# A four-layer attention and MLP kernel: VectorE and GpSimd exchange work, each GpSimd step tied to a VectorE sum, and the order plan spares time after transfers

## The chip, the cores and the metric

The kernel runs on one core of a Trainium2 chip. The metric is the device time of one execution in microseconds (us); three runs of the kernel before gave 1188.9 us as their median (1188.76 to 1190.28).

## The reference

```python
x = A_x                                               # 1 x 2048 x 640
x = x + A(layernorm(x), wqkv, wo)                     # attention, 32 heads of 20
x = x + B(layernorm(x), w1, b1, w2, b2)               # B has a layernorm of its own
x = x + A(layernorm(x), wqkv, wo)                     # the same weights again
x = x + B(layernorm(x), w1, b1, w2, b2)
# A: q, k, v = x @ wqkv; every position attends to itself and to 7 earlier ones, 2 apart;
#    softmax over these 8; the weighted sum of v; then @ wo
# B: gelu(y @ w1 + b1) @ w2 + b2, with 1536 hidden columns
```

## The kernel before, in words

**Units.** The even and the odd positions never meet in the attention, so the 2048 rows are cut into four units of 512 rows (two of even, two of odd positions). Two layers make eight units, n = 0 to 7; units 4 to 7 are the second layer. A unit has four row tiles t and four head groups g (8 heads, 160 columns each).

**Products in two halves.** Every fp32 operand of a product is split into a high and a low fp16 half, and each product is three fp16 passes on TensorE. ScalarE rounds the high half; the low half is a subtraction of 640 elements per partition, as a rule on VectorE: line 506 for the normalised rows `hl`, line 653 for the attention's result `ohl`, lines 720 and 849 for the hidden rows.

**Stages of a unit.** (1) The layernorm: sums on ScalarE, a power of -0.5 on GpSimd (line 487), low halves (line 506), then a transposing DMA into `yT` (line 511). (2) The product with `wqkv` (line 539), evicted by ScalarE into `ev` (three buffers) and put into DRAM in another layout by a DMA from ScalarE's queue (line 551); it is fetched again by SyncE (line 570). (3) The attention of each group on VectorE: products of q and k in two halves of 2560 elements (line 606), each summed by a TENSOR_REDUCE (line 610), the softmax (lines 615 to 625), the products with v (line 632), three adding steps (lines 640 and 644) into the one buffer `o`, then the high half (line 651, ScalarE) and the low half (line 653). (4) After the fourth group, four transposing DMAs (line 661) and the projection with `wo` (line 672, 120 matmuls, called the project below); VectorE adds it to x (line 678). (5) The second layernorm, and the bias b2 added to x (line 515, VectorE, 640 elements for each of the 32 tiles). (6) The MLP: the first product (line 709), gelu and halves (lines 715, 718, 720), the second product (lines 728 and 731), and the sum into x (line 751).

**The last two units.** For units 6 and 7 the second MLP product is done in a Strassen form with seven products instead of eight (`mlp_fast`): first products at line 834 (180 matmuls a unit), seven products at line 900 (252 matmuls a unit), sums into x at line 919. It needs sums of weights, made once by `prep_sums` (line 776: 24 operations of 320 elements and 6 of 1280, on GpSimd), and sums of hidden rows (line 854: 24 operations of 256 elements a unit; unit 6 on GpSimd, unit 7 on VectorE).

**What sets the order.** All steps are handed to a `Plan` with an engine, a duration, a priority, what they need and give, and the buffers that they use. `Plan.run` plays them through once on the host, always takes the step that can start first (with ties by priority), and the kernel then emits them in order of their planned start. Each engine works through its own list in that order on the chip; a step that is late there holds all that stands behind it. DMA commands stand in such lists too: SyncE's list (SP) holds nearly all, ScalarE's the puts (line 551) and the split weights on their way to DRAM (24 `mw` transfers, line 410 now).

Of the kernel before, what the change touches and what calls it, by code (L numbers as in the profile page):

```python
# [45 lines left out]

FAST_OUT = (6, 7)
# [16 lines left out]
class Plan:  # L64
# [12 lines left out]

    PATIENCE = 0.7
# [12 lines left out]
    def add(self, eng, dur, prio, emit, need=(), give=(), use=(), table=None, move=0.0, lazy=False):  # L91
        o = dict(eng=eng, dur=dur, prio=prio, emit=emit, need=need, give=give, use=use, table=table,
                 move=move, lazy=lazy, n=len(self.ops))
        self.ops.append(o)
        for u in use:
            if u not in self.users and u[0] in self.ORDERED and u not in self.line.setdefault(u[0], []):
                self.line[u[0]].append(u)
            self.users[u] = self.users.get(u, 0) + 1

    def run(self):  # L100
# [13 lines left out]
        order = []  # L114

        def start(o):
# [3 lines left out]
            for k in o["need"]:  # L120
                e, w = when[k]
                w = w + (self.LAG[e] if e != o["eng"] else 0.06 * (e != "pe"))
                t = max(t, w)
            new = {}
            for u in o["use"]:
                if u in self.slot:
                    t = max(t, self.since[u])
                else:
# [7 lines left out]
                    new[u[0]] = i + 1  # L136
            return t

        total = len(self.ops)
        while len(order) < total:  # L140
# [19 lines left out]
            d = o["dur"]  # L160
            if o["table"] and o["table"] != table:
# [23 lines left out]
            for k in o["give"]:  # L185
                when[k] = (e, end)
# [19 lines left out]
def sliding_dilated_then_mlp_kernel(  # L206
# [76 lines left out]
    T["g"] = [b[:, :NS * HT2].rearrange("p (s c) -> p s c", s=NS) for b in (act_buf, ev_buf)]  # L283
# [27 lines left out]
    def dve(n, prio, emit, need=(), give=(), use=(), more=0.0):  # L311
        plan.add("dve", v_cost(n) + more, prio, emit, need, give, use)
# [3 lines left out]

    def dma(kb, prio, emit, need=(), give=(), use=(), by="sp"):
        lazy = give[0][0] in ("x", "sq", "st", "c1", "c2", "zero", "mw", "tr", "ms", "fw") or give[0] in ("b1", "b2")
        plan.add(by, 0.1 if by == "act" else 0.38, prio, emit, need, give, use, move=kb / 330.0, lazy=lazy)

    def dma_transpose(prio, emit, need=(), give=(), use=()):
        plan.add("sp", 1.45, prio, emit, need, give, use, move=1.4)
# [5 lines left out]
    def constants():  # L328
        nc.vector.memset(half, -0.5)
# [6 lines left out]
    def mask_value():  # L336
        nc.vector.tensor_scalar(mask, mask, 0.0, -1e9 / scale, op0=OP.is_lt, op1=OP.mult)
# [67 lines left out]
    def prep_m(f, i, prio):  # L405
# [4 lines left out]
        dma(328, prio - 5, lambda: nc.scalar.dma_start(mw[i][f], tile_of(*ck)),  # L410
            need=[("lo", ("m", f, i))], give=[("mw", f, i)], use=[ck], by="act")

    def turn(prio, t, name, hk, yk):

        for a in range(2):
# [27 lines left out]
    def layernorm(n, prio, yk, twice):  # L443
# [13 lines left out]
        for t in range(m if fast else 0):  # L457
            def stats(t=t):
# [3 lines left out]
                nc.vector.tensor_scalar_add(bn[:, t, 13:14], bn[:, t, 13:14], EPS)  # L462
# [19 lines left out]
        for t0 in range(0, 0 if fast else m, cut):  # L482
# [4 lines left out]
            pool(2.5, prio, lambda t0=t0, t1=t1: nc.gpsimd.tensor_tensor(  # L487
# [6 lines left out]
        for t in range(m):  # L494
# [19 lines left out]
            if twice:  # L514
                dve(D, -350, lambda t=t: nc.vector.tensor_add(x[u][:, t], x[u][:, t], b2),  # L515
                    need=[("y", name, t), ("fg", n, 2, 0) if n in FAST_OUT else ("hhi", at(n, t) * NF + 2 * t + 2), "b2"], give=[("xb", n, t)])

# [3 lines left out]
    def qkv(n):  # L521
# [6 lines left out]
        for k, (g, b) in enumerate(halves):  # L528
            ek = ("ev", (n, g, b))
            for i in range(2):  # L530
# [12 lines left out]
                mm(3 * KD * 3 * GC, 15, -500 + n + 0.01 * k, product,  # L543
# [5 lines left out]
            def put(g=g, b=b, ek=ek):  # L549
                to = spill[la][par]  # L550
                nc.scalar.dma_start(
# [5 lines left out]
                give=[("put", n, g, b)], use=[ek], by="act")  # L557
# [20 lines left out]
    def attention(G):  # L578
# [21 lines left out]
        for a in range(NE):  # L600
# [3 lines left out]
            def qk(t0=t0, pk=pk):  # L604
                w = tile_of(*wk)
                nc.vector.tensor_mul(tile_of(*pk), w[:, HALO + m + t0:HALO + m + t0 + EH, None, :].to_broadcast([P, EH, W, GC]),  # L606
# [5 lines left out]
                axis=AX.X, op=OP.add), need=[("qk", G, a)], give=[("lg", G, a)], use=[pk, sk])  # L612
# [14 lines left out]
        for a in range(NE):  # L627
# [3 lines left out]
            def pv(t0=t0, vk=vk):  # L631
                nc.vector.tensor_mul(  # L632
# [15 lines left out]
        def hi():  # L648
# [4 lines left out]
        dve(m * GC, -300 + G, lambda: nc.vector.tensor_sub(tile_of(*hk)[:, :, 1, g * GC:(g + 1) * GC], tile_of(*ok), hi()),  # L653
            need=[("oh", G)], give=[("ol", G)], use=[ok, hk])

    def project(n):
# [7 lines left out]
        for t in range(m):  # L664
            for c in range(2):
# [10 lines left out]
                def residual(t=t, c=c, pk=pk):  # L676
                    xs = x[u][:, t, c * D // 2:(c + 1) * D // 2]
                    nc.vector.scalar_tensor_tensor(xs, tile_of(*pk)[:, :D // 2], 1.0 / WS, xs, op0=OP.mult, op1=OP.add)  # L678
# [8 lines left out]
    def mlp(at, b, t0, t1):  # L687
# [61 lines left out]
        def residual(c0, c1, i0, i1, src):  # L749
            xt = x[u][:, i0:i1, c0:c1]  # L750
            nc.vector.scalar_tensor_tensor(xt, src, 1.0 / WS, xt, op0=OP.mult, op1=OP.add)
# [10 lines left out]
    def prep_sums(j, prio):  # L762
# [12 lines left out]
        def add(o, a, b, op):  # L775
            nc.gpsimd.tensor_tensor(o, a, b, op=op)  # L776
# [5 lines left out]
        def t1():  # L782
            b11, b12, b21, b22, tf = blocks_of()
            add(tf[:, 1], b12, b11, OP.subtract)

        def t3():
            b11, b12, b21, b22, tf = blocks_of()
            add(tf[:, 2], b22, b12, OP.subtract)

        def t2():  # L790
            b11, b12, b21, b22, tf = blocks_of()
            add(tf[:, 0], b22, tf[:, 1], OP.subtract)

        def t4():
            b11, b12, b21, b22, tf = blocks_of()
            add(tf[:, 3], b21, tf[:, 0], OP.subtract)
# [4 lines left out]
        for name, f, need in (("1", t1, both), ("3", t3, both), ("2", t2, [("ts", j, "1")]), ("4", t4, [("ts", j, "2")])):  # L801
            pool(1.0, prio, f, need=need, give=[("ts", j, name)], use=[key])
        act(4 * HD, -300, lambda: nc.scalar.activation(parts()[2][:, :, 0], parts()[1], AF.Copy),
            need=[("ts", j, "4"), ("ts", j, "3")], give=[("th", j)], use=[key])
        pool(3.2, prio, lambda: add(parts()[2][:, :, 1], parts()[1], parts()[2][:, :, 0], OP.subtract),
             need=[("th", j)], give=[("tl", j)], use=[key])
# [4 lines left out]
    def mlp_fast(at, b):  # L811
# [4 lines left out]
        free = [("out", b - 1, NF - 1, i) for i in range(M)] if b - 1 not in FAST_OUT else []  # L816
        free += [("ms", q, j) for q in SUMS for j in range(HF)] + [("put", N - 1, g, i) for g in range(NG) for i in range(2)]
# [4 lines left out]
        for jj in range(HF):  # L822
            gk, hk = ("g", (b, jj)), ("h", (b, jj))
            for s in range(2):
# [20 lines left out]
            def split_h(half, low, gk=gk, hk=hk):  # L845
                s0, s1 = ((0, 3), (3, NS))[half]
                to = tile_of(*hk)[half]
                if low:
                    nc.vector.tensor_sub(to[:, 1], gs(gk, s0, s1), to[:, 0])
# [3 lines left out]
            def add(o, a, c, op, gk=gk):  # L853
                (nc.vector if b == N - 1 else nc.gpsimd).tensor_tensor(tile_of(*gk)[:, o], tile_of(*gk)[:, a], tile_of(*gk)[:, c], op=op)
# [3 lines left out]
            for i, (o, a, c, op) in enumerate(((4, 3, 1, OP.add), (5, 4, 2, OP.subtract), (6, 0, 5, OP.subtract), (3, 2, 3, OP.subtract))):  # L858
                f = lambda o=o, a=a, c=c, op=op, f=add: f(o, a, c, op)
                if b == N - 1:  # L860
# [139 lines left out]
```

## Time and profile before

| | us |
|---|---|
| median of 3 runs | 1188.9 |
| the profiled execution | 1189.57 |
| its span, first to last instruction | 1187.8 |
| TensorE (PE) busy | 1153.7 |
| VectorE (DVE) busy | 1063.6 |
| ScalarE (ACT) busy | 538.3 |
| GpSimd (POOL) busy | 153.0 |

Busy times are of the span. PE waits in the trace are idle times ahead of an instruction, put down to what came last. A row of the timeline has its start, its length, the engine, the line, what it writes and reads, how many like it follow each other, and in brackets the idle time ahead of it.

### The profile page before, as it was taken

What the parts mean: (1) busy time and instruction counts of PE and PEld (TensorE: products, weight loads), DVE (VectorE), ACT (ScalarE), POOL (GpSimd) and SP (SyncE); (2) the same over time, 40 slices, a digit from 0 to 9 for tenths busy, and PEclk for the clock granted to TensorE, in tenths of its full rate; (3) what the DMA queues carried; (4) which work ended last, traced back from release to release, by engine and by line L of the source; (5) the groups of instructions that cost most, each with busy time, mean ns of one, the idle gap of its engine ahead of it and who ended that gap; (6) DMA issues with size and microseconds to landing.
All of it is one profiled execution on the core that took longest, in us unless ns stands there. A gap on an engine that the chain in (4) does not pass through costs nothing.

```text
span 1187.8 us, 17373 instructions
## 1 busy us (share of the span) xinstructions
PE 1153.7 (97%) x6844; PEld 632.0 (53%) x6844; DVE 1063.6 (90%) x1030; ACT 538.3 (45%) x939; POOL 153.0 (13%) x100
## 2 busy tenths in 40 slices
PE   7999999999979999999999999999998799989998
PEld 4444446577544565545554455546454555447556
DVE  7899999999999999999998999989999999873361
ACT  6476444535283435732637253364343552344240
POOL 1011000001010000000002010022055440450000
PEclk9999999999999999999999999999999899989999
DMA  9998999889675558577565757568766894546645
GB/s 303 289 314 271 309 328 279 244 264 289 172 218 161 175 170 205 164 195 207 153 199 150 203 152 210 182 159 175 212 237 238 231 241 130 183 100 187 182 124 173
DMA packets 235758, 248.77 MB, mean 209 GB/s; under 512 B 131148, under 2 KB 185756, under 8 KB 235676
## 3 DMA queue, kind: packets, MB, share of 16 engines
q1 hardware_dynamic: 206620, 208.34, 61.5%
q10 hardware_dynamic: 29056, 39.33, 9.5%
q8 instruction: 53, 0.87, 0.3%
q14 instruction: 29, 0.24, 0.1%
HBM read 168.76 MB, written 48.71 MB: 183 GB/s over the span
## 4 chain that ended last, share of the span: by engine, by line
PE 66%; DVE 21%; issue 6%; POOL 3%; ACT 2%; DMA 2%; SPq 0%; DVEq 0%; POOLq 0%; ACTq 0%
PE ps L539 25%; PE ps L709 12%; PE acc L728 9%; PE ps L672 8%; PE acc L900 6%; DVE pr L606 4%; DVE pr L632 4%; PE ps L834 3%; DVE pr L640 3%; DVE sm L610 3%; PE acc L731 2%; POOL ln L487 2%; DVE act L720 2%; DVE xf L515 1%; DVE hl L506 1%
## 5 line engine op out<-in xcount | busy, mean ns | idle before, releaser
L539 PE MATMUL ps<-wq,yT 128*128 128x480 f16 x1920 | 392.6, 367 | 0.0
L539 PEld LDWEIGHTS <-yT 128*128 128x128 f16 x1920 | 187.9, 98 | 201.2 <-issue 1.5
L709 PE MATMUL ps<-yT,c 128*128 128x512 f16 (+1 forms) x1260 | 248.8, 351 | 6.4 <-DMA yT<-hl 6.4
L728 PE MATMUL acc<-c,act 128*128 128x512 f16 x864 | 240.4, 379 | 2.4 <-DVE act L720 2.3
L632 DVE TENSOR_TENSOR pr<-sm,v 128x2560 f32<-128x2560 f32 x64 | 182.4, 2868 | 0.0
L709 PEld LDWEIGHTS <-c 128*128 128x128 f16 x1260 | 120.7, 98 | 114.7 <-issue 9.9
L606 DVE TENSOR_TENSOR pr<-qk 128x2560 f32<-128x2560 f32 x64 | 179.6, 2807 | 0.1
L610 DVE TENSOR_REDUCE sm<-pr 128x128 f32<-128x2560 f32 x64 | 179.6, 2806 | 0.0
L731 PE MATMUL acc<-c,act 128*128 128x128 f16 x864 | 178.6, 219 | 0.9 <-DVE act L720 0.9
L487 POOL TENSOR_TENSOR ln<-ln,half 128x2 f32<-128x2 f32 (+1 forms) x30 | 58.2, 1938 | 761.1 <-ACT ln L484 761.1
L672 PE MATMUL ps<-wo,yT 128*128 128x320 f16 x960 | 136.7, 305 | 14.2 <-DMA yT<-ohl 12.4
L545 ACT ACTIVATE ev<-ps 128x480 f32<-128x480 f32 x128 | 72.3, 566 | 170.3 <-PE ps L539 169.9
L640 DVE TENSOR_TENSOR pr<-pr 128x640 f32<-128x640 f32 (+1 forms) x128 | 148.7, 1184 | 0.0
L728 PEld LDWEIGHTS <-act 128*128 128x128 f16 x864 | 84.2, 98 | 101.0 <-DVE act L720 3.7
L672 PEld LDWEIGHTS <-yT 128*128 128x128 f16 x960 | 95.4, 100 | 55.9 <-DMA yT<-ohl 14.2
L715 ACT ACTIVATE act<-ps,b 128x512 f32<-128x512 f32 (+1 forms) x84 | 52.1, 623 | 156.4 <-PE ps L709 148.1
L731 PEld LDWEIGHTS <-act 128*128 128x128 f16 x864 | 82.0, 98 | 8.9 <-DVE act L720 1.0
L834 PE MATMUL ps<-yT,c 128*128 128x512 f16 x360 | 78.5, 379 | 0.4 <-ACT act L840 0.3
L470 ACT ACTIVATE junk<-xf 128x640 f16<-128x640 f32 x56 | 41.2, 735 | 81.6 <-DVE xf L678 71.4
L720 DVE TENSOR_TENSOR act<-act 128x512 f16<-128x512 f32 (+1 forms) x84 | 58.0, 693 | 15.2 <-ACT act L718 15.1
L776 POOL TENSOR_TENSOR wq<-wq 128x320 f32<-128x320 f32 (+1 forms) x30 | 56.4, 1898 | 67.8 <-ACT wq L798 47.4
L900 PE MATMUL acc<-c,wq 128*128 128x320 f16 x420 | 61.8, 299 | 0.0
(82 smaller groups left out, 942.0 us busy)
## 6 DMA issues: line engine op xcount, KB each, us to landing
c<-mw SPq DMA_DIRECT2D x192, 320.0 KB, 3.4
spill<-ev ACTq DMA_DIRECT2D x64, 480.0 KB, 4.2
qk<-spill SPq DMA_DIRECT2D x32, 880.0 KB, 6.2
v<-spill SPq DMA_DIRECT2D x32, 880.0 KB, 4.9
qk<-spill SPq DMA_DIRECT2D x32, 320.0 KB, 4.0
mw<-c ACTq DMA_DIRECT2D x24, 320.0 KB, 4.7
c<-msp SPq DMA_DIRECT2D x24, 320.0 KB, 3.5
act<-in_B_w_dram SPq DMA_DIRECT2D x21, 320.0 KB, 5.6
```

Source lines behind the costliest of these rows:

```text
L487: pool(2.5, prio, lambda t0=t0, t1=t1: nc.gpsimd.tensor_tensor(col(2)[:, t0:t1], col(2)[:, t0:t1], half[:, t0:t1], op=OP.pow), need=[("vr" ...
L539: nc.tensor.matmul(ps, transposed(yk)[:, a * KD + k, t * P:(t + 1) * P], wq[:, b, k, g], start=j == 0, stop=j == 3 * KD - 1)
L606: nc.vector.tensor_mul(tile_of(*pk), w[:, HALO + m + t0:HALO + m + t0 + EH, None, :].to_broadcast([P, EH, W, GC]), windows(w, t0, [GC, W], ...
L610: dve(E, G - 0.7, lambda pk=pk, t0=t0: nc.vector.tensor_reduce(lg(t0, t0 + EH).rearrange("p t w h -> p (t w h)"), tile_of(*pk).rearrange(" ...
L632: nc.vector.tensor_mul(tile_of(*vk).rearrange("p t w (h d) -> p t (w h) d", d=DH), lg(t0, t0 + EH).rearrange("p t w h -> p t (w h)")[:, :, ...
L640: dve(EH * w * GC, G - 0.9, lambda vk=vk, w=w: nc.vector.tensor_add(tile_of(*vk)[:, :, 0:w], tile_of(*vk)[:, :, 0:w], tile_of(*vk)[:, :, w ...
L672: nc.tensor.matmul(tile_of(*pk)[:, :D // 2], transposed(yk)[:, a * KD + k, t * P:(t + 1) * P], wo[:, b, k, c * D // 2:(c + 1) * D // 2], s ...
L709: nc.tensor.matmul(tile_of(*pk)[:, :nt], tile_of(*ck)[:, a, k * P:(k + 1) * P], transposed(yk)[:, c * KD + k, t0 * P:t1 * P], start=i == 0 ...
L728: nc.tensor.matmul(acc[i], w, tile_of(*wk)[:, c, :BANK], start=e == 0 and (a, c) == PASS[0], stop=end, skip_group_check=True)
L731: nc.tensor.matmul(acc[4][:, i * P:(i + 1) * P], w, tile_of(*wk)[:, c, BANK:], start=e == 0 and i == t0 and (a, c) == PASS[0], stop=end, s ...
L834: nc.tensor.matmul(tile_of(*pk), tile_of(*ck)[:, a, k * P:(k + 1) * P], transposed(yk)[:, c * KD + k, :], start=i == 0, stop=i == 3 * KD - 1)
L900: nc.tensor.matmul(acc[bank][:, :HD], tile_of(*hk)[half][:, a, slot, t * P:(t + 1) * P], load()[:, z, c], start=q in FIRST and i == 0 and ...
```

## The change

The edits, none of which alters what is computed:

1. **GpSimd to VectorE.** The 30 sums of weights (line 776 before, 815 now) and the 24 sums of hidden rows of unit 6 (line 854 before, 894 now) go to VectorE.
2. **VectorE to GpSimd.** The low half of `ohl` for groups 0 to 2 of each unit (24 of 32; line 653 before, 689 now) and the bias additions of units 0 to 6 (28 of 32; line 515 before, 548 now) go to GpSimd.
3. **Ties.** Such a step (`laid`) is planned into a window: the time of a TENSOR_REDUCE of line 610 (646 now). It then waits, by an added dependency, for the VectorE instruction just ahead of that sum, so that it starts when the sum starts. If no window is to be had in time, it is planned without a tie. Of the 52 steps 46 are tied; not tied are one bias addition of unit 0, the four of unit 6 and the low half of group 2 of unit 7.
4. **Spared time.** In the plan a TensorE step that needs a transfer counts it as landed 0.5 us later, and 2.0 us later for a transposing DMA.
5. **Queues.** The 64 puts and the 24 `mw` transfers go from ScalarE's queue to SyncE's.
6. **Smaller ones.** The first product of unit 4 gets a late priority; the planned length of the power on GpSimd is 3.0 instead of 2.5; the two buffers `g` of the Strassen form change places, so that the first of them needn't wait for unit 5's outputs.

```diff
+SPARE = (0.5, 2.0)
...
+        def window(o, t):
+            for w in windows:
+                if o["beside"] > w[3]:
+                    continue
+                s = max(t, w[0])
+                if s + o["dur"] <= w[1] + self.OVER:
+                    return s, w
+            return None, None
...
-                w = w + (self.LAG[e] if e != o["eng"] else 0.06 * (e != "pe"))
+                w = w + (self.LAG[e] if e != o["eng"] else 0.06 * (e != "pe")) + spare * (o["eng"] == "pe")
...
+                if o["opens"]:
+                    shut -= 1
+                    windows.append([t + 0.2, t + d, ahead, o["opens"]])
+                    del windows[:-4]
...
-    T["g"] = [b[:, :NS * HT2].rearrange("p (s c) -> p s c", s=NS) for b in (act_buf, ev_buf)]
+    T["g"] = [b[:, :NS * HT2].rearrange("p (s c) -> p s c", s=NS) for b in (ev_buf, act_buf)]
...
+    def laid(n, prio, emit, until, need=(), give=(), use=(), level=1):
+        plan.add("pool", 0.17 + n / 450.0, prio, emit, need, give, use, beside=level, until=until)
...
-                mm(3 * KD * 3 * GC, 15, -500 + n + 0.01 * k, product,
+                mm(3 * KD * 3 * GC, 15, (-500 + n if n != NU else 24 + 11 * b) + 0.01 * k, product,
...
-                nc.scalar.dma_start(
+                nc.sync.dma_start(
...
-        dve(m * GC, -300 + G, lambda: nc.vector.tensor_sub(tile_of(*hk)[:, :, 1, g * GC:(g + 1) * GC], tile_of(*ok), hi()),
-            need=[("oh", G)], give=[("ol", G)], use=[ok, hk])
+        low = lambda by: by.tensor_tensor(tile_of(*hk)[:, :, 1, g * GC:(g + 1) * GC], tile_of(*ok), hi(), op=OP.subtract)
+        if g < NG - 1:
+            laid(m * GC, -300 + G, lambda: low(nc.gpsimd), lambda ready, when: any(("o", G + 1) in q["use"] for q in ready.get("dve", ())), need=[("oh", G)], give=[("ol", G)], use=[ok, hk])
+        else:
+            dve(m * GC, -300 + G, lambda: low(nc.vector), need=[("oh", G)], give=[("ol", G)], use=[ok, hk])
...
-            nc.gpsimd.tensor_tensor(o, a, b, op=op)
+            return nc.vector.tensor_tensor(o, a, b, op=op)
...
     for o in plan.run():
-        o["emit"]()
+        o["ins"] = o["emit"]()
+        if o["behind"]:
+            tc.add_manual_dep(o["ins"].ins, o["behind"]["ins"].ins.name, mybir.DependencyInfo(
+                mybir.DependencyClass.Sync, mybir.DependencyReason.DATA), reason="order")
```

GpSimd's list near the last units, before: powers of layernorms (`ln`), then the sums of weights (`wq` is the buffer that these share).

```order
L487 TENSOR_TENSOR ln_91<-ln_91,half 128x2 x2
L487 TENSOR_TENSOR ln_90<-ln_90,half 128x2 x2
L487 TENSOR_TENSOR ln_89<-ln_89,half 128x2 x2
L487 TENSOR_TENSOR ln_91<-ln_91,half 128x2 x2
L487 TENSOR_TENSOR ln_90<-ln_90,half 128x2 x2
L776 TENSOR_TENSOR wq<-wq 128x320 x4
L776 TENSOR_TENSOR wq<-wq 128x4x320
```

GpSimd's list now, at its end: low halves (`ohl`) and bias additions (`xf`) between the last powers.

```order
L548 TENSOR_TENSOR xf<-xf,b_103 128x640
L520 TENSOR_TENSOR ln_89<-ln_89,half 128x2 x2
L548 TENSOR_TENSOR xf<-xf,b_103 128x640
L689 TENSOR_TENSOR ohl_73<-o_86,ohl_73 128x4x160
L548 TENSOR_TENSOR xf<-xf,b_103 128x640
L689 TENSOR_TENSOR ohl_73<-o_86,ohl_73 128x4x160
L548 TENSOR_TENSOR xf<-xf,b_103 128x640 x5
L689 TENSOR_TENSOR ohl_73<-o_86,ohl_73 128x4x160
L520 TENSOR_TENSOR ln_91<-ln_91,half 128x2 x2
```

The sums have left GpSimd; powers of layernorms now stand behind tied steps, and the last low half of GpSimd stands behind five bias additions.

VectorE's list at the last group of unit 7 before: products with v and adding steps (`pr`, `o`), between them low halves and bias additions of unit 6 (`wq`, `xf`), and the last low half of the attention (`ohl`), on which the project of unit 7 waits.

```order
L632 TENSOR_TENSOR pr_75<-sm_88,v_69 128x2560
L849 TENSOR_TENSOR wq<-act,wq 128x768
L849 TENSOR_TENSOR wq<-act,wq 128x1024
L640 TENSOR_TENSOR pr_74<-pr_74 128x2x640
L640 TENSOR_TENSOR pr_75<-pr_75 128x2x640
L849 TENSOR_TENSOR wq<-ev,wq 128x768
L849 TENSOR_TENSOR wq<-ev,wq 128x1024
L515 TENSOR_TENSOR xf<-xf,b_103 128x640 x4
L849 TENSOR_TENSOR wq<-act,wq 128x768
L849 TENSOR_TENSOR wq<-act,wq 128x1024
L640 TENSOR_TENSOR pr_74<-pr_74 128x2x320
L640 TENSOR_TENSOR pr_75<-pr_75 128x2x320
```

The same place now, up to the last low half and the first steps behind it (`acc` are PSUM banks of unit 5).

```order
L790 SCALAR_TENSOR_TENSOR xf<-acc_98,xf 128x512
L676 TENSOR_TENSOR pr_75<-pr_75 128x2x320
L676 TENSOR_TENSOR pr_74<-pr_74 128x2x640
L680 TENSOR_TENSOR o_86<-pr_75 128x320
L676 TENSOR_TENSOR pr_74<-pr_74 128x2x320
L680 TENSOR_TENSOR o_86<-pr_74 128x320
L689 TENSOR_TENSOR ohl_73<-o_86,ohl_73 128x4x160
L894 TENSOR_TENSOR ev<-ev 128x256 x4
L889 TENSOR_TENSOR wq<-ev,wq 128x768
L889 TENSOR_TENSOR wq<-ev,wq 128x1024
```

The low halves of unit 6 and its bias additions no longer stand ahead of the last low half. On TensorE the project of unit 7 stood behind all 180 first products (line 834) of unit 6; now it stands behind 75 of them, and the other 105 follow it. The project of unit 6 stood behind the first products of three hidden blocks of unit 5 (45 matmuls of line 709) and 30 pairs of second products (lines 728 and 731) that now follow it.

More of the change, by code (lines that the diff above doesn't have):

```diff
@@ L76 @@
     LAND = 1.0
+    OVER = 0.3
     PATIENCE = 0.7
@@ L89, in __init__, with add @@
         self.line = {}
-    def add(self, eng, dur, prio, emit, need=(), give=(), use=(), table=None, move=0.0, lazy=False):
+    def add(self, eng, dur, prio, emit, need=(), give=(), use=(), table=None, move=0.0, lazy=False, spare=0.0,
+            opens=0, beside=0, until=None):
         o = dict(eng=eng, dur=dur, prio=prio, emit=emit, need=need, give=give, use=use, table=table,
-                 move=move, lazy=lazy, n=len(self.ops))
+                 move=move, lazy=lazy, spare=spare, opens=opens, beside=beside, until=until, behind=None, ins=None, n=len(self.ops))
         self.ops.append(o)
@@ L114, in run @@
         order = []
+        windows = []
+        shut = sum(o["opens"] > 0 for o in self.ops)
+        ahead = None
+        def window(o, t):
[6 more added lines that the diff above has]
+            return None, None
         def start(o):
@@ L136, in start @@
                     new[u[0]] = i + 1
+            if o["beside"] and (shut or windows):
+                s, _ = window(o, t)
+                return s if s is not None or shut and not o["until"](ready, when) else t
             return t
@@ L160, in run @@
             d = o["dur"]
+            if o["beside"]:
+                _, w = window(o, t)
+                if w:
+                    w[0] = t + d + 0.1
+                    o["behind"] = w[2]
+            if e == "dve":
+                if o["opens"]:
+                    shut -= 1
+                    windows.append([t + 0.2, t + d, ahead, o["opens"]])
+                    del windows[:-4]
+                ahead = o
             if o["table"] and o["table"] != table:
@@ L328, in constants @@
     def constants():
-        nc.vector.memset(half, -0.5)
+        return nc.vector.memset(half, -0.5)
     dve(8, -900, constants, give=["half"])
@@ L556, in qkv @@
             dma(P * 6 * GC * 4 / 1e3, -310 + n, put, need=[("ev", n, 2 * b + i, g) for i in range(2)],
-                give=[("put", n, g, b)], use=[ek], by="act")
+                give=[("put", n, g, b)], use=[ek])
     def fetch(G):
@@ L815, in mlp_fast @@
         ready = [("yT", ("b", b), t) for t in range(M)]
-        free = [("out", b - 1, NF - 1, i) for i in range(M)] if b - 1 not in FAST_OUT else []
-        free += [("ms", q, j) for q in SUMS for j in range(HF)] + [("put", N - 1, g, i) for g in range(NG) for i in range(2)]
+        free = [("ms", q, j) for q in SUMS for j in range(HF)] + [("put", N - 1, g, i) for g in range(NG) for i in range(2)]
         def gs(k, s0, s1):
@@ L823, in mlp_fast @@
             gk, hk = ("g", (b, jj)), ("h", (b, jj))
+            if jj == 1 and b - 1 not in FAST_OUT:
+                free += [("out", b - 1, NF - 1, i) for i in range(M)]
             for s in range(2):
```

66 lines of the change are left out of this document (33 added, 33 removed).

## The prediction

> **What bounds the kernel now.** I read the page's busy times first, then TensorE's waits, then the timeline at the longest of them.
>
> ```profile
> PE 1153.7 (97%) x6844; PEld 632.0 (53%) x6844; DVE 1063.6 (90%) x1030; ACT 538.3 (45%) x939; POOL 153.0 (13%) x100
> ```
>
> TensorE is busy for 97% of the span, and the change neither adds nor removes a matmul. All that can be won is TensorE's idle time, with what hangs on it.
>
> ```profile
> PE ps L672 <- DMA yT<-ohl: 12.4, 3, 6.8
> PE ps L709 <- DMA yT<-hl: 6.4, 1, 6.4
> PE acc L728 <- DVE act L720: 2.3, 3, 0.9
> PE ps L672 <- DVE xf L678: 1.8, 1, 1.8
> PE acc L731 <- DVE act L720: 0.9, 1, 0.9
> PE ps L834 <- ACT act L840: 0.3, 1, 0.3
> ```
>
> Each row: who waited for whom, us in total, times, the longest. They sum to 24.1 us; the start-up, which the change hardly touches, has the rest. The largest part is the project (line 672), which waits for the transposed low halves of the attention three times. The timeline of TensorE shows these waits in brackets, and the same work without a wait for comparison (the first row, and the last one, from the chain of work that ended last).
>
> ```profile
> 192.59 16.46 PE L672 MATMUL ps<-wo,yT 128*128 128x320 f16 x120
> 355.11 7.12 PE L709 MATMUL ps<-yT,c 128*128 128x512 f16 x22 [6.43 <-DMA yT<-hl]
> 680.14 10.12 PE L672 MATMUL ps<-wo,yT 128*128 128x320 f16 x72 [1.63 <-DMA yT<-ohl]
> 925.33 8.39 PE L672 MATMUL ps<-wo,yT 128*128 128x320 f16 x45 [6.83 <-DMA yT<-ohl]
> 1057.62 18.98 PE L672 MATMUL ps<-wo,yT 128*128 128x320 f16 x120 [3.89 <-DMA yT<-ohl]
> 1114.14 35.61 PE ps L834 x165
> ```
>
> After a long wait TensorE also runs slow for a while. A project's 120 matmuls take 16.46 us with no wait ahead of them and 18.98 behind the 3.89 us wait: 2.5 us lost. The 45 behind 6.83 us take 8.39 instead of 45 x 16.46 / 120 = 6.2: 2.2 lost. The 22 behind 6.43 us take 7.12 instead of 22 x 35.61 / 165 = 4.7: 2.4 lost. The 72 behind 1.63 us take 10.12 against 9.9: nothing. The granted clock (the column before the last two) shows it:
>
> ```profile
> 315.00:430.00 115.00, 107.67 (x638) 58.44 (x637) 111.76 (x106) 55.08 (x94) 3.49 (x3) 0.97 0.64 186
> 900.00:960.00 60.00, 51.30 (x316) 28.95 (x315) 60.00 (x53) 29.94 (x50) 32.13 (x17) 0.94 0.84 248
> ```
>
> So the waits cost 24.1 + 7.1 = 31.2 us, and that is the ceiling of any gain. [...]
>
> The second row of that answer also shows VectorE busy for all 60 us. It is the partner that TensorE waits for: the low half of the last group of a unit ends its attention.
>
> ```profile
> 1053.27 0.83 DVE L653 TENSOR_TENSOR ohl<-o,ohl 128x640 f16<-128x640 f32 x1 [0.80 <-ACT ohl L651]
> ```
>
> It starts at 1053.27 and the project at 1057.62, 4.35 us later, by way of the transposing DMA. The question is how much earlier VectorE gets there, and how much earlier TensorE.
>
> **VectorE's list, part by part.** Groups by line and shape: count, busy us, mean ns of one, idle time ahead.
>
> ```profile
> L653 DVE TENSOR_TENSOR ohl<-o,ohl 128x640 f16<-128x640 f32 x32 | 27.6, 862 | 3.0 <-ACT ohl L651 3.0
> L515 DVE TENSOR_TENSOR xf<-xf,b 128x640 f32<-128x640 f32 x32 | 29.2, 925 | 0.0
> L644 DVE TENSOR_TENSOR o<-pr 128x320 f32<-128x320 f32 x64 | 32.7, 521 | 0.0
> L849 DVE TENSOR_TENSOR wq<-act,wq 128x1024 f16<-128x1024 f32 x6 | 7.3, 1223 | 5.5 <-ACT wq L851 5.5
> L849 DVE TENSOR_TENSOR wq<-act,wq 128x768 f16<-128x768 f32 x6 | 6.8, 1125 | 0.0
> L854 DVE TENSOR_TENSOR act<-act 128x256 f32<-128x256 f32 x12 | 4.8, 423 | 6.4 <-ACT act L840 6.2
> L506 DVE TENSOR_TENSOR hl<-y,hl 128x640 f16<-128x640 f32 x64 | 51.4, 818 | 7.3 <-ACT hl L504 7.3
> L720 DVE TENSOR_TENSOR act<-act 128x512 f16<-128x512 f32 x60 | 48.2, 804 | 14.0 <-ACT act L718 13.9
> L720 DVE TENSOR_TENSOR act<-act 128x256 f16<-128x256 f32 x24 | 9.7, 416 | 1.3 <-ACT act L718 1.2
> L632 DVE TENSOR_TENSOR pr<-sm,v 128x2560 f32<-128x2560 f32 x64 | 182.4, 2868 | 0.0
> L606 DVE TENSOR_TENSOR pr<-qk 128x2560 f32<-128x2560 f32 x64 | 179.6, 2807 | 0.1
> ```
>
> Ahead of the last low half of unit 7, VectorE loses 24 low halves, 24 x 0.862 = 20.7 us; 28 bias additions, 28 x 0.925 = 25.9; and three pairs of low halves of unit 6's hidden rows, which now stand behind it, 3 x (1.125 + 1.223) = 7.0. It gains 24 weight sums of 320 elements, priced at the row of that shape, 24 x 0.521 = 12.5, and 6 of 1280, by the 1024 row scaled up, 6 x 1.53 = 9.2. The 24 sums of hidden rows (24 x 0.424 = 10.2) stand behind it, beside TensorE's own work, and I cost them at nothing (10.2 if that cover fails). Net: 53.6 - 21.7 = 31.9 us earlier.
>
> **The contention that goes.** Some operations of VectorE are stretched while GpSimd makes its sums, others not. GpSimd's timeline, then VectorE's:
>
> ```profile
> 861.47 3.45 POOL L776 TENSOR_TENSOR wq<-wq 128x320 f32<-128x320 f32 x4 [31.50 <-ACT wq L798]
> 867.15 4.16 POOL L776 TENSOR_TENSOR wq<-wq 128x1280 f16<-128x1280 f32 x1 [2.23 <-ACT wq L803]
> 899.91 2.62 POOL L776 TENSOR_TENSOR wq<-wq 128x1280 f16<-128x1280 f32 x1 [1.38 <-ACT wq L803]
> 861.90 2.81 DVE L610 TENSOR_REDUCE sm<-pr 128x128 f32<-128x2560 f32 x1
> 866.02 7.96 DVE L632 TENSOR_TENSOR pr<-sm,v 128x2560 f32<-128x2560 f32 x2
> 899.34 2.81 DVE L610 TENSOR_REDUCE sm<-pr 128x128 f32<-128x2560 f32 x1
> ```
>
> Two TENSOR_TENSORs of line 632 beside a GpSimd sum take 3.98 us each against a mean of 2.87, and that sum takes 4.16 against 2.62 beside a TENSOR_REDUCE. The TENSOR_REDUCE takes 2.81 beside GpSimd's sums. So a GpSimd step beside that sum costs VectorE nothing, and a step of 640 elements there is between 0.86 us (320) and 2.62 (1280), by a line through both 1.45: it ends inside the 2.81. That is what the ties aim at.
>
> What the contention costs before, from the groups: line 515 against line 506 of the same size, 32 x (0.925 - 0.818) = 3.4 us; line 653 likewise 32 x 0.044 = 1.4; line 720 at 512 elements against 0.684 by a line through its 256 and line 506's 640, 60 x 0.120 = 7.2; line 632 against 606, 64 x 0.061 = 3.9. Sum 15.9. All could be contention (15.9) or, if the operations differ by themselves, little of it (0). I take 15.9, since the two stretched operations above alone show 2.2.
>
> Of this some comes back: the steps without a tie. Unit 6's four bias additions and unit 7's low half of group 2 run in the last group, beside TENSOR_TENSORs: 5 x 1.45 = 7.2 us at most, which I charge in full.
>
> VectorE's last low half: 31.9 + 15.9 - 7.2 = 40.6 us earlier.
>
> **TensorE's side.** It gets to the project of unit 7 earlier by the 105 first products that now follow it, 105 x 35.61 / 165 = 22.7 us, by the waits before, 24.1 - 3.9 = 20.2, and by the slow stretches behind them, 2.2 + 2.4 = 4.6: 47.5 us, at 1057.62 - 3.89 - 47.5 = 1006.2. The transposed rows come at 1057.62 - 40.6 = 1017.0. So by rows alone that wait does not go; it grows to 10.8 us. But VectorE waited too:
>
> ```profile
> DVE xf L678 <- PE ps L672: 13.5, 16, 2.1
> DVE act L720 <- ACT act L718: 15.1, 20, 4.0
> ```
>
> The residual sums of the projects (line 678) waited 13.5 us for TensorE, which was late by its own waits, and line 720 waited 15.1 for ScalarE. With 2.0 us spared after each transposing DMA, TensorE has other work at those places, and I expect a third of the 28.6, some 9 us, to go; none of it to all of it is possible. Then the rows come at 1008 and the wait is about 2 us.
>
> **The sum.** From the project of unit 7 on, TensorE has 1187.8 - 1057.62 = 130.2 us before, 2.5 of it slow clock; now 127.7 + 22.7 = 150.4. The span is 1008 + 150.4 = 1158.4 with nothing else late. Waits at other places (the project of unit 3, ahead of which the order takes 60 first and 78 second products from TensorE, has the least to spare) delay TensorE but not VectorE, so they count only where they outlast the 2 us; I add 5 us for them and one slow stretch: 1163.4. The profiled execution is 1.8 over its span (1189.57) and 0.7 over the median, so 1164.5 in the median; I say **1165**.
>
> **The other edits.** Late priority of unit 4's first product: it is spread between MLP products. Between the project of unit 1 and the 6.4 us wait of line 709 for that unit's layernorm stood 15 matmuls of line 539, 45 half-wide ones of line 709 and 60 second products; now 105 of line 539 and 36 second products stand there.
>
> ```profile
> L539 PE MATMUL ps<-wq,yT 128*128 128x480 f16 x1920 | 392.6, 367 | 0.0
> ```
>
> That is 90 x 0.204 = 18.4 us more and, by the rates above, 45 x 0.108 + 24 x 0.137 = 8.1 less: 10.3 us of cover for 6.4. The change of `g` lets unit 6 start its gelu before unit 5's outputs are done: nothing, or a part of the 0.3. The queues: 88 more commands in SyncE's list, which mostly waits.
>
> ```profile
> SPq L570 <- DVE pr L632: 137.7, 26, 11.0
> L551 ACTq DMA_DIRECT2D spill<-ev x64: 365/367/418, 23.0 to 859.7; - x64
> DMA to landing us min/median/max: 2.7/4.2/9.7
> ```
>
> A put costs 0.37 us to issue and lands in 4.2 (at most 9.7). With three buffers `ev` and one filled in 30 matmuls of 0.204 us, 6.1 us, a put may be some 5 us late at the worst landing before ScalarE has no buffer. A put behind a fetch that waits 11.0 us would stall line 539. I take nothing, and up to 10 us for the range.
>
> **Rivals.** *TensorE alone bounds* (0.14): VectorE's waits go altogether, all 31.2 us are won, 1157.7. For it: 28.6 us of waits on VectorE; against it: the 10.8 us above.
>
> *VectorE stays the bound* (0.13): the 15.9 us aren't contention, or come back, and its waits stay. Then the rows come at 1057.62 - 24.7 = 1032.9 and the span is 1032.9 + 150.4 + 2.5 = 1185.8: 1187 in the median; half of it gives 1176.
>
> *The ties bind the wrong way, slower* (0.11). GpSimd works through its list in order, and powers of layernorms stand behind tied steps.
>
> ```profile
> 779.57 8.02 POOL L487 TENSOR_TENSOR ln<-ln,half 128x2 f32<-128x2 f32 x1 [4.50 <-ACT ln L484]
> ```
>
> A power of two elements took 8.02 us here beside VectorE's TENSOR_TENSORs: GpSimd gets no turn. A tied step that comes late by ScalarE's high half misses its sum, and then costs VectorE 1.45 us, or waits as long as this. If every tied step missed, 46 x 1.45 = 66.7 us go; from about 17 misses (25 us) the gain is spent, and half of them missing gives 1165 + 33 = 1198. Against it: the sum is 1.36 us longer than the step. [...]
>
> *It doesn't do what it says* (0.04): the waits just change places, within 0.2%.
>
> **The numbers.** Forecast 0.58, 1159 to 1175. Faster by over 0.2% (2.4 us, about what a measurement of this kernel tells from no change) are the forecast, the first rival and most of the second: 0.85. Same 0.04, slower 0.11. The range reaches from the ceiling, 1157, to 1183, where 0.04 of the second rival, the same and the slower case are left out.
>
> **What would show it.** Right: TensorE's waits in the middle of the trace under 10 us in all, TENSOR_REDUCEs of 2.81 us beside GpSimd's steps, line 720 near 0.69 us, the project of unit 7 starting near 1010 us. Wrong: TensorE waiting for GpSimd or for `ev`; line 632 over 2.9 us; powers of many us ahead of idle TensorE; a project of unit 7 later than 1034 us.

## The result, and the profile after

The changed kernel takes 1158.4 us (median of 4 runs, 1157.31 to 1159.81) against 1189.59 for the kernel before on the same chip: a ratio of 0.9736, 95% interval 0.9719 to 0.9753. The forecast was 1165, its range 1157 to 1183; the time lies at its lower end, beside the first rival's 1157.7 (TensorE alone bounds). The page of the changed kernel begins:

```profile
span 1156.5 us, 17451 instructions
...
PE 1145.4 (99%) x6844; PEld 630.5 (55%) x6844; DVE 1033.0 (89%) x1032; ACT 539.2 (47%) x939; POOL 128.9 (11%) x98
...
PEclk9999999999999999999999999999999999999999
```

The span is 31.3 us shorter. TensorE's busy time fell by 8.3 us with the same matmuls, since the slow stretches behind long waits are gone: the row of granted clock before, `PEclk9999999999999999999999999999999899989999`, has two slices at 8, and none is left now. Its waits in the middle of its list, 22.4 us less, account for nearly all of the rest. These are all that are left:

```profile
PE acc L770 <- DVE act L759: 0.8, 1, 0.8
PE acc L767 <- DMA c<-mw: 0.6, 1, 0.6
PE ps L748 <- DMA c<-mw: 0.3, 1, 0.3
```

1.7 us instead of 24.1. No project waits for its transposed rows any more. The last low half of the attention and the project of unit 7, from the timelines of VectorE and TensorE:

```profile
999.02 0.82 DVE L689 TENSOR_TENSOR ohl<-o,ohl 128x640 f16<-128x640 f32 x1 [0.80 <-ACT ohl L687]
1006.70 16.46 PE L711 MATMUL ps<-wo,yT 128*128 128x320 f16 x120
```

The low half stands 54.3 us earlier than before (1053.27) and the project 50.9. There are 7.7 us between them where the way takes 4.35, so 3.3 us are in hand, and the 120 matmuls run at the full 16.46 us. All four signs that the prediction named for being right are there: few waits in the middle (1.7 us), TENSOR_REDUCEs of line 646 at 2.80 us, line 759 (720 before) at 694 ns, and the project of unit 7 near 1010 us.

The groups on VectorE (first five rows) and GpSimd (last two) that were priced, and the adding step that the sum of the contention left out (line 680, 644 before):

```profile
L759 DVE TENSOR_TENSOR act<-act 128x512 f16<-128x512 f32 x60 | 41.6, 694 | 7.4 <-ACT act L757 6.9
L668 DVE TENSOR_TENSOR pr<-sm,v 128x2560 f32<-128x2560 f32 x64 | 180.5, 2837 | 0.0
L680 DVE TENSOR_TENSOR o<-pr 128x320 f32<-128x320 f32 x64 | 30.1, 481 | 0.0
L815 DVE TENSOR_TENSOR wq<-wq 128x320 f32<-128x320 f32 x24 | 10.6, 479 | 0.0
L815 DVE TENSOR_TENSOR wq<-wq 128x1280 f16<-128x1280 f32 x6 | 8.9, 1481 | 0.0
L548 POOL TENSOR_TENSOR xf<-xf,b 128x640 f32<-128x640 f32 x28 | 44.1, 1581 | 212.6 <-DVE sm L661 138.9 <-DVE sm L660 55.5 <-DVE pr L676 12.2
L689 POOL TENSOR_TENSOR ohl<-o,ohl 128x640 f16<-128x640 f32 x24 | 33.6, 1402 | 327.3 <-DVE sm L655 166.3 <-DVE sm L659 103.3 <-ACT ohl L687 21.6
```

Line 759 (720 before) has fallen from 804 to 694 ns, and a GpSimd step takes 1.40 to 1.58 us where 1.45 was forecast. One tied step and the TENSOR_REDUCE beside it, from the two timelines:

```profile
953.26 1.40 POOL L689 TENSOR_TENSOR ohl<-o,ohl 128x640 f16<-128x640 f32 x1 [18.70 <-DVE sm L659]
953.03 2.81 DVE L646 TENSOR_REDUCE sm<-pr 128x128 f32<-128x2560 f32 x1
```

It starts 0.23 us behind the TENSOR_REDUCE's start, ends inside it, and the TENSOR_REDUCE takes the 2.81 us that it took before. All 46 tied steps do so: in the trace each starts 0.15 to 0.61 us behind a TENSOR_REDUCE of line 646. Five bias additions that GpSimd does one behind another near the end of its list, the last four without a tie, show the other case:

```profile
964.52 8.57 POOL L548 TENSOR_TENSOR xf<-xf,b 128x640 f32<-128x640 f32 x5 [9.87 <-DVE pr L676]
...
964.37 2.81 DVE L646 TENSOR_REDUCE sm<-pr 128x128 f32<-128x2560 f32 x1
968.32 1.29 DVE L759 TENSOR_TENSOR act<-act 128x512 f16<-128x512 f32 x1 [1.15 <-ACT act L757]
969.53 2.16 DVE L676 TENSOR_TENSOR pr<-pr 128x640 f32<-128x640 f32 x1
971.61 4.16 DVE L668 TENSOR_TENSOR pr<-sm,v 128x2560 f32<-128x2560 f32 x1
```

The first two still run beside the TENSOR_REDUCE. Beside the other three, VectorE's next TENSOR_TENSORs, against 0.69, 0.84 and 2.84 us in the mean, lose 0.6, 1.3 and 1.3 us. The fifth step without a tie in this last group, the low half at 980.75, falls where VectorE does nothing.

### The profile page after: what moved, and what is told of

The parts are those of the page before. It is cut to its first block, busy times and chain, and to the rows that moved or that the text cites. A ratio compares the mean times of both kernels' runs of the same rounds, so it can differ in the third digit from the quotient of the medians.

```text
span 1156.5 us, 17451 instructions
## 1 busy us (share of the span) xinstructions
PE 1145.4 (99%) x6844; PEld 630.5 (55%) x6844; DVE 1033.0 (89%) x1032; ACT 539.2 (47%) x939; POOL 128.9 (11%) x98
## 4 chain that ended last, share of the span: by engine, by line
PE 95%; DMA 2%; DVE 1%; issue 1%; ACT 1%; SPq 0%; DVEq 0%
PE ps L575 34%; PE ps L748 19%; PE acc L767 14%; PE ps L711 11%; PE ps L874 7%; PE acc L937 6%; PE acc L770 4%; DMA c<-mw 2%; DMA pr<-in_A_wqkv_dram 1%; DVE pr L676 0%; DVE act L759 0%; DVE hl L539 0%; ACT hl L537 0%; ACT L657 0%; PE acc L457 0%
## 5 line engine op out<-in xcount | busy, mean ns | idle before, releaser
L748 PE MATMUL ps<-yT,c 128*128 128x512 f16 (+1 forms) x1260 | 246.1, 349 | 0.3 <-DMA c<-mw 0.3
L676 DVE TENSOR_TENSOR pr<-pr 128x1280 f32<-128x1280 f32 (+1 forms) x128 | 145.1, 1159 | 0.0
L711 PE MATMUL ps<-wo,yT 128*128 128x320 f16 x960 | 131.7, 299 | 0.0
L520 POOL TENSOR_TENSOR ln<-ln,half 128x2 f32<-128x2 f32 (+1 forms) x30 | 44.6, 1486 | 328.4 <-ACT ln L517 327.0
L689 POOL TENSOR_TENSOR ohl<-o,ohl 128x640 f16<-128x640 f32 x24 | 33.6, 1402 | 327.3 <-DVE sm L655 166.3
L548 POOL TENSOR_TENSOR xf<-xf,b 128x640 f32<-128x640 f32 x28 | 44.1, 1581 | 212.6 <-DVE sm L661 138.9
```

Of the source, the lines that this page charges most:

```text
L676: dve(EH * w * GC, G - 0.9, lambda vk=vk, w=w: nc.vector.tensor_add(tile_of(*vk)[:, :, 0:w], tile_of(*vk)[:, :, 0:w], tile_of(*vk)[:, :, w ...
L711: nc.tensor.matmul(tile_of(*pk)[:, :D // 2], transposed(yk)[:, a * KD + k, t * P:(t + 1) * P], wo[:, b, k, c * D // 2:(c + 1) * D // 2], s ...
L748: nc.tensor.matmul(tile_of(*pk)[:, :nt], tile_of(*ck)[:, a, k * P:(k + 1) * P], transposed(yk)[:, c * KD + k, t0 * P:t1 * P], start=i == 0 ...
```

## The experiments

The theory was that VectorE, relieved of load and of GpSimd's contention, is what made the gain; the rivals were the spared time, the work exchange in any form, and the queues. All times are medians of 4 runs; each ratio is to the kernel before, measured beside it on the same chip; the changed kernel's is 0.9736.

**Spared time alone**, in the kernel before.

```diff
-                w = w + (self.LAG[e] if e != o["eng"] else 0.06 * (e != "pe"))
+                w = w + (self.LAG[e] if e != o["eng"] else 0.06 * (e != "pe")) + spare * (o["eng"] == "pe")
```

> The kernel before with the spared time in its plan and nothing else. By the order VectorE's work ahead of the projects stays within 7 us. Theory (VectorE was late by its load and by the contention): the waits move, TensorE still waits 10 to 25 us, 1175 to 1190. Rival (the waits were the plan's optimism on transfers): TensorE's waits fall under 5 us, 1158 to 1165.

1180.83 us, ratio 0.9914 (0.9886 to 0.9942). The theory's case: the waits move to other places. The longest two:

```profile
PE acc L730 <- DVE xf L753: 10.4, 1, 10.4
PE ps L711 <- DMA yT<-hl: 4.9, 1, 4.9
```

The first is a second product that waits for VectorE to empty its PSUM bank: VectorE is late, only elsewhere. So the spare by itself is worth some 9 us.

**The change without spared time** (and with the early priority of unit 4's first product).

```diff
-SPARE = (0.5, 2.0)
+SPARE = (0.0, 0.0)
...
-                mm(3 * KD * 3 * GC, 15, (-500 + n if n != NU else 24 + 11 * b) + 0.01 * k, product,
+                mm(3 * KD * 3 * GC, 15, -500 + n + 0.01 * k, product,
```

> The changed kernel with no time spared in the plan (0.0 and 0.0 instead of 0.5 and 2.0 us), and with the early priority of unit 4's first product again, since without spare the late one leads the plan into a dead end. By the order, TensorE gets to the projects of units 4, 6 and 7 with 6, 9 and 4 us less work ahead than in the changed kernel, VectorE does the same work as there. Theory (the relief of VectorE made the gain, the spare only picks up the last us): the projects had 3 to 5 us in hand, so waits of 1 to 5 us come back at units 4, 6 and 7, with one slow stretch: 1161 to 1169. Rival (the spared time made the gain): most of the 24 us of waits come back, 1178 to 1190.

1158.05 us, 0.9735 (0.9705 to 0.9765): nothing lost, less than the theory allowed, and the rival is out. Two edits were taken back here, so by itself this run says only that the gain doesn't need the two together; the next one parts them.

**The early priority alone**, with the spare.

```diff
-                mm(3 * KD * 3 * GC, 15, (-500 + n if n != NU else 24 + 11 * b) + 0.01 * k, product,
+                mm(3 * KD * 3 * GC, 15, -500 + n + 0.01 * k, product,
```

> The changed kernel with the early priority of unit 4's first product, with the spare; it parts the two edits of the run without spare. Theory (neither edit counts once VectorE is relieved): 1156 to 1162. Rival (one is worth some us and the other costs as much): outside that, on either side, by 4 us or more.

1162.25 us, 0.9775 (0.9756 to 0.9795). It lies 0.25 us outside the theory's range, some 4 us over the run without spare and 4 us over the changed kernel. Taken as they stand, the spare costs 4 us here and the late priority gives 4 back. That is the rival's picture, short of the size that it asked for; the intervals of this run and the one before just overlap. Whether it is the edits or only where the order happens to fall wasn't followed further. Neither makes the gain.

**The low halves and bias additions back on VectorE.**

```diff
-        if g < NG - 1:
+        if False:
...
-                if n == N - 1:
+                if True:
```

> The changed kernel with the 52 low halves and bias additions back on VectorE; the sums stay on VectorE, so GpSimd has only its powers and there is no contention. VectorE has 52 x 0.82 = 43 us more. The plan answers by putting all of unit 6's products ahead of the project of unit 7, so that nothing of unit 6 is left to cover unit 7's layernorm. Theory (moving this work away from VectorE is a needed part): 20 to 25 us of waits, most of them behind the last project: 1175 to 1190. Rival (getting rid of the contention is enough): 1157 to 1164.

1177.69 us, 0.9891 (0.9869 to 0.9913), as the theory had it, at the place that it named:

```profile
PE ps L874 <- DMA yT<-hl: 12.9, 1, 12.9
```

TensorE waits for unit 7's layernorm with nothing of unit 6 left to do. In a plan made for it, taking GpSimd's contention away without taking work off VectorE is not enough. The last low half comes at 1060.42 here, 7 us later than in the kernel before, and the kernel is still 12 us faster than that one, so part of the gain lies in the order that the other edits give. The run wasn't repeated in the changed kernel's order, so how much of the 19 us lost is order isn't shown.

**The sums back on GpSimd**, planned there.

```diff
-            dve(HD, prio, f, need=need, give=[("ts", j, name)], use=[key])
+            pool(1.0, prio, f, need=need, give=[("ts", j, name)], use=[key])
```

and likewise for the sums of 1280 elements and for unit 6's hidden rows.

> The changed kernel with the 30 weight sums and the 24 sums of unit 6's hidden rows back on GpSimd (the planned lengths of before), with the tied steps on GpSimd too. VectorE has 20 us less ahead of the last project, but the untied sums run beside its TENSOR_TENSORs, some 15 us of contention, and in GpSimd's list they stand behind tied steps and these behind them. Theory (contention and order on GpSimd cost what the shorter VectorE list gives): 1160 to 1175, line 759 at 512 elements back near 0.80 us. Rival (the sums on VectorE are no part of the gain): 1157 to 1160 and 0.69.

1180.93 us, 0.9929 (0.991 to 0.9947): slower than both expectations. Its page, its longest waits, VectorE's last low half and its project of unit 7:

```profile
PE 1151.7 (98%) x6844; PEld 633.7 (54%) x6844; DVE 1034.1 (88%) x978; ACT 538.5 (46%) x939; POOL 214.5 (18%) x152
...
PE acc L767 <- DVE xf L790: 8.9, 1, 8.9
PE ps L711 <- DMA yT<-ohl: 6.0, 2, 4.3
...
998.57 0.83 DVE L689 TENSOR_TENSOR ohl<-o,ohl 128x640 f16<-128x640 f32 x1 [0.80 <-ACT ohl L687]
1003.01 9.18 PE L711 MATMUL ps<-wo,yT 128*128 128x320 f16 x54 [4.34 <-DMA yT<-ohl]
```

VectorE has 54 operations fewer and is busy as long as with them (1034.1 against 1033.0), and its last low half comes at the same time. What 54 operations would take (10.6 + 8.9 + 24 x 0.423 = 29.7 us) is lost again, which is put down to contention; line 759 at 512 elements takes 766 ns, between the 694 and the 0.80 us of the two expectations, and 60 x 0.072 = 4.3 us of it are that line's. And the plan, whose lengths of steps are fixed and know nothing of that, has put the last project 125 matmuls further forward in TensorE's list, so TensorE arrives early and waits.

**The same, in the changed kernel's order**: planned as on VectorE, emitted to GpSimd.

```diff
-            return nc.vector.tensor_tensor(o, a, b, op=op)
+            return nc.gpsimd.tensor_tensor(o, a, b, op=op)
...
-                return nc.vector.tensor_tensor(tile_of(*gk)[:, o], tile_of(*gk)[:, a], tile_of(*gk)[:, c], op=op)
+                return (nc.vector if b == N - 1 else nc.gpsimd).tensor_tensor(tile_of(*gk)[:, o], tile_of(*gk)[:, a], tile_of(*gk)[:, c], op=op)
```

> The changed kernel with the weight sums and unit 6's hidden sums emitted to GpSimd, but planned as if VectorE did them: the order of TensorE is that of the changed kernel. In the run that planned them on GpSimd, VectorE was busy as long as in the changed kernel with 54 operations fewer, and its last low half came at the same time (998.6 against 999.0), while TensorE's list had the last project 23 us earlier. Theory (the loss there was the order, planned without the contention): 1158 to 1166. Rival (the loss was GpSimd being slow with the sums or holding up the powers behind them): 1172 to 1185.

1165.85 us, 0.9805 (0.9787 to 0.9822): the theory's case. Of the 22.5 us between the run above and the changed kernel, some 15 are the order (of all engines' lists) and some 7 the sums' place itself. VectorE is busy for 1019.7 us here:

```profile
PE 1147.6 (99%) x6844; PEld 631.5 (54%) x6844; DVE 1019.7 (88%) x978; ACT 538.1 (46%) x939; POOL 204.3 (18%) x152
```

that is 13.3 less than in the changed kernel for 29.7 us of work less. The 16 us between are put down to contention: the groups that both kernels have on VectorE, each by its mean here against there, show 13.0 of them (line 759 at 512 elements 757 against 694 ns, 3.8 us; line 680 539 against 481, 3.7 us).

**No ties**, the same order.

```diff
-                    o["behind"] = w[2]
+                    o["behind"] = None
```

> The changed kernel without the added dependencies: the 46 steps stand in the same place of GpSimd's list, but start as soon as their inputs are there and the step before is done. Theory (a step beside a TENSOR_REDUCE is free, beside a TENSOR_TENSOR it costs VectorE up to 1.4 us): some of them start early, beside TENSOR_TENSORs; 10 to 30 of them cost 1 to 1.4 us each, of which 3 us are in hand: 1165 to 1190. Rival (the ties do nothing, the plan alone or the lighter VectorE list is enough): 1157 to 1161.

1163.98 us, 0.9776 (0.9753 to 0.9798). Between the cases, just under the theory's: the ties are worth some 5 us. VectorE is busy 11.7 us longer (first row), and GpSimd's low half takes twice as long (second row):

```profile
PE 1146.3 (99%) x6844; PEld 630.8 (54%) x6844; DVE 1044.7 (90%) x1032; ACT 538.3 (46%) x939; POOL 181.0 (16%) x98
...
L689 POOL TENSOR_TENSOR ohl<-o,ohl 128x640 f16<-128x640 f32 x24 | 67.1, 2796 | 338.9 <-ACT ohl L687 329.1 <-issue 9.8
```

**Ties at the products** instead of the TENSOR_REDUCEs.

```diff
-give=[("qk", G, a)], use=[wk, pk, sk])
+give=[("qk", G, a)], use=[wk, pk, sk], opens=1 + a)
...
-give=[("lg", G, a)], use=[pk, sk], opens=1 + a)
+give=[("lg", G, a)], use=[pk, sk])
```

> The changed kernel with the windows and ties at the product ahead of the TENSOR_REDUCE (line 642, a TENSOR_TENSOR of the same 2560 elements) instead of at the TENSOR_REDUCE itself. The same work, the same number of ties. Theory (a TENSOR_TENSOR contends with GpSimd's reads): line 642 goes from 2.80 to about 3.8 us in the mean, 46 x 1.4 = 64 us more for VectorE, 1195 to 1225. Rival (what matters is only that the steps are ordered, not what they run beside): line 642 stays at 2.80 to 2.85 and the time at 1157 to 1165.

1162.73 us, 0.9771 (0.9751 to 0.9791). The theory failed, and the rival's numbers held, though not its reason: what the steps run beside does matter. That it is GpSimd's reads with which a TENSOR_TENSOR contends, as the theory has it, no run shows. VectorE's product and GpSimd's two groups:

```profile
L642 DVE TENSOR_TENSOR pr<-qk 128x2560 f32<-128x2560 f32 x64 | 180.6, 2825 | 2.5 <-DMA qk<-spill 2.5
L548 POOL TENSOR_TENSOR xf<-xf,b 128x640 f32<-128x640 f32 x28 | 99.5, 3565 | 154.3 <-DVE sm L660 108.7 <-DVE sm L659 31.7 <-DVE sm L661 11.5
L689 POOL TENSOR_TENSOR ohl<-o,ohl 128x640 f16<-128x640 f32 x24 | 95.9, 3994 | 318.5 <-ACT ohl L687 186.9 <-DVE sm L660 60.4 <-DVE sm L655 36.0
```

The contention is there, but the product doesn't pay it: its mean is 2.825 instead of 2.802. GpSimd's steps take 3.6 to 4.0 us instead of 1.4 to 1.6. One of them, and VectorE beside it:

```profile
339.71 3.99 POOL L548 TENSOR_TENSOR xf<-xf,b 128x640 f32<-128x640 f32 x1 [3.81 <-DVE sm L660]
...
339.55 2.76 DVE L642 TENSOR_TENSOR pr<-qk 128x2560 f32<-128x2560 f32 x1
342.23 1.75 DVE L661 TENSOR_TENSOR sm<-sm 128x256 f32<-128x256 f32 x1
```

The step ends 1.39 us behind the product's end, about its usual length (1.55 is the median in the changed kernel), as if it had waited for that. The next TENSOR_TENSOR takes 1.75 us beside it, where line 661 takes 0.41 in the mean of the changed kernel, and ends 0.28 us behind the step. So VectorE pays with the operations behind, line 759 at 875 ns instead of 694, and was busy 25.9 us longer as a whole (1058.9), not the 64 expected. In the trace 41 of the 52 steps start in the first 0.8 us of a product of line 642. And the order differed here: the plan had the project of unit 7 some 19 us further back in TensorE's list, which took up part of that.

**Plain steps on GpSimd**, neither windows nor ties.

```diff
-        plan.add("pool", 0.17 + n / 450.0, prio, emit, need, give, use, beside=level, until=until)
+        plan.add("pool", 0.17 + n / 450.0, prio, emit, need, give, use)
```

> The changed kernel with the 52 steps given to GpSimd as plain steps: neither window nor tie, planned as soon as they are ready. About one quarter of VectorE's attention time is the TENSOR_REDUCE, so some three quarters of the steps fall beside TENSOR_TENSORs. Theory: 35 to 40 of them cost VectorE 1 to 1.4 us each, 35 to 55 us, or GpSimd waits as long: 1180 to 1215. Rival (handing the work to GpSimd in any way gives the gain): 1157 to 1165.

1161.17 us, 0.9764 (0.974 to 0.9787): the rival held. Handing the 52 steps to GpSimd in this plain way gives all but 3 us of the gain, and the interval overlaps the changed kernel's. VectorE is busy 17.7 us longer (1050.7), half of what the theory took as its least. Its order, too, has the project of unit 7 some 19 us further back, so it tells less of the ties than the run without them in the same order, which lost 5.6.

**Puts on ScalarE's queue**, planned there.

```diff
-                nc.sync.dma_start(
+                nc.scalar.dma_start(
...
-                give=[("put", n, g, b)], use=[ek])
+                give=[("put", n, g, b)], use=[ek], by="act")
```

and likewise for the 24 weight transfers.

> The changed kernel with the 64 puts and 24 weight transfers issued from ScalarE's queue again. Theory (the queues are no part of the gain): 1156 to 1163, with no new wait over 2 us. Rival (ScalarE's queue or the order of the puts made part of it): over 1165.

1164.77 us, 0.9793 (0.9775 to 0.981): between the two, with a 2.7 us wait for a layernorm among the new ones. To part queue and order:

**The same in the changed kernel's order.**

```diff
-                nc.sync.dma_start(
+                nc.scalar.dma_start(
```

and likewise for the 24 weight transfers.

> The changed kernel with puts and weight transfers issued from ScalarE's queue, but planned as on SyncE's: the lists of TensorE, VectorE and GpSimd are those of the changed kernel. Theory (the 6 us of the run that planned them on ScalarE's queue were its order): 1157 to 1161. Rival (the queue itself): 1163 to 1168.

1158.99 us, 0.9751 (0.9731 to 0.9771): the queue itself counts for nothing that can be told here, the 6 us were the order.

**Without the bias additions**; the output lacks b2.

```diff
-                last = lambda by, t=t: by.tensor_tensor(x[u][:, t], x[u][:, t], b2, op=OP.add)
+                last = lambda by, t=t: None
```

> The changed kernel with the bias additions of b2 left out (32 steps, 28 of them on GpSimd; the output lacks b2 twice), in the same order. Theory (TensorE's own work sets the time now, VectorE and GpSimd have a few us in hand): 1155 to 1160. Rival (GpSimd or VectorE still bounds): under 1152.

1155.87 us, 0.9727 (0.9707 to 0.9747), 2.5 us less than the changed kernel with overlapping intervals, as the theory had it. GpSimd has 46 us less work and the time hardly moves: TensorE's own work, busy for 99% of the span, bounds now.

## Why the prediction was right, and where it was off

- *What bounds.* Right. The ceiling of 31.2 us was the right account: the span fell by 31.3, the waits by 22.4 and TensorE's busy time by 8.3. The slow stretch behind long waits was 7.1 in the sum and about 8 in fact.
- *TensorE's side.* Right. It was to reach the project of unit 7 at 1006.2 without waits; it started it at 1006.70.
- *VectorE's list.* Right: 31.9 us less was forecast; with the measured 0.479 and 1.481 us of the sums it is 53.6 - 24 x 0.479 - 6 x 1.481 = 33.2.
- *The contention that goes.* Its largest term was right in size: line 720 was to lose 0.120 us at each of 60, and lost 0.110. The rest of this part was off in both directions. The sum counts 28 x 0.107 + 24 x 0.044 = 4.1 us twice: the bias additions and low halves that leave VectorE were taken off at their full, stretched lengths, and the stretch was then taken off again. The adding steps were left out and lost 5.8: line 644 went from 32.7 to 30.1, line 640 from 149.9 to 146.7. Line 632 was to lose 3.9 and lost 1.9. And the 7.2 for the steps without a tie was too much: three stretched operations show 3.2.
- *VectorE's own waits.* Right in size, wrong in where. VectorE's busy and idle time ahead of the last low half, before and now (its own busy time is the third after the comma):

```profile
0.00:1053.27 1053.27, 1026.91 (x6039) 552.60 (x6040) 1009.66 (x944) 498.86 (x878) 143.99 (x90) 0.99 0.73 215
...
0.00:999.02 999.02, 991.25 (x5900) 538.28 (x5901) 964.04 (x915) 488.56 (x863) 127.40 (x96) 1.00 0.76 224
```

  It was idle for 1053.27 - 1009.66 = 43.6 us before and is for 35.0 now: 8.6 less, where 9 was forecast. But the two rows that the 9 was taken from didn't both shrink. Up to the low half these are the waits, before and now:

```profile
DVE act L720 <- ACT act L718: 15.1, 20, 4.0
DVE hl L506 <- ACT hl L504: 6.4, 7, 2.2
DVE xf L678 <- PE ps L672: 3.9, 8, 0.8
...
DVE act L759 <- ACT act L757: 7.7, 18, 1.1
DVE hl L539 <- ACT hl L537: 2.7, 5, 0.8
DVE xf L717 <- PE ps L711: 6.6, 12, 1.1
```

  The residual sums' 13.5 us lie for the most part behind the low half, which they can't delay there; the 3.9 ahead of it grew to 6.6. Line 720 gave 7.4, and the layernorm's low halves, which weren't named, 3.7. That the total met the 9 is partly luck.
- *The low half.* It was to come 40.6 + 9 = 49.6 us earlier and came 54.3 earlier: 45.6 by work and contention, 8.6 by idle time. The 5.0 us more lie in the first part, in the terms of the contention that were mis-sized.
- *The 7 us of waits left over.* Wrong: 2 at the last project and 5 at others were expected; the project had none and 1.7 remain in all. The span was to be 1163.4 and is 1156.5: the 5 that weren't needed, 1.3 by which the project starts ahead of the 1008 in the sum, and 0.6 behind it make the 6.9.
- *The rivals.* TensorE alone as the bound had 0.14, and the time is its time. Its reason isn't what happened: VectorE's waits didn't go altogether, 35.0 us of idle time stayed, and its list became shorter instead. VectorE as the bound is out: its transposed rows landed at 1003.35, not 1032.9, and line 720's stretch went. The slower one failed in its condition, since no tied step missed its TENSOR_REDUCE, and its price holds only where GpSimd comes first: there a VectorE operation lost up to 1.3 us, but the product that a step was tied to lost 0.02 in the mean. The prediction's own row had it already: the two operations of line 632 read as 3.98 us each are one of 2.81, begun at 866.02, ahead of GpSimd's sum (867.15), and one of 5.23, begun behind it at 868.75.
- *What was not seen.* The prediction asked how much VectorE gains by the exchange. The experiments say that the plan's ignorance of contention counts as well: sums put back on GpSimd cost VectorE 16 to 31 us, where they save it 29.7, the plan counts only what they save, and the order built on that is worth some 15 of the 22.5 us between the sums' two places. That the kernel before lost in the same way is likely, but no run moves the sums there alone.

The parts don't add up by themselves: spare alone gives 9 us in the kernel before and no gain in the changed one; taking back either half of the work exchange, planned anew, loses 19 to 22 us of the 31, and taking back the sums in the same order loses 7.

## What to carry to other kernels

In a kernel whose order is planned ahead, a cost that the plan doesn't know can be paid twice: once where it arises (7 us here), and once by every engine that was told to be early for it (15 us here). Work that one engine cannot hide from another belongs where the plan's price for it is true, even on the busier of the two. Once the engine that all wait for is at 99%, queues, spare and ties were worth some 5 us at most here, about as much as two plans that hardly differ.

## What the runs showed of the hardware

In the steps and sums shown here, who paid for the contention between VectorE and GpSimd went by who came first; the power of 8.02 us in the kernel before, which outlasted eight TENSOR_TENSORs, doesn't fit that. In the changed kernel a GpSimd step of 640 elements took 1.40 us (low half) or 1.55 (bias addition, the median) beside a TENSOR_REDUCE, which stayed at 2.81. With ties at the products, at the start of a TENSOR_TENSOR of 2.8 us, such a step took 3.57 (bias additions) and 3.99 (low halves) in the mean, and the TENSOR_TENSOR was stretched by only 0.02 us in the mean; the TENSOR_TENSOR behind it took 1.75 us instead of 0.41 in the case shown. Beside a chain of steps on GpSimd, one behind another, VectorE's next operations in the changed kernel took 0.6, 1.3 and 1.3 us longer than their means.

In the kernel before, a wait of 3.9 to 6.8 us cost TensorE another 2.2 to 2.5 us of slow matmuls behind it; one of 1.6 us cost nothing.
